# Feed-forward products of a fp32 attention and feed-forward kernel, issued in column pieces of at most 192

## The chip, the cores and the metric

The kernel runs on one core of a Trainium2 chip. The metric is the device time of one execution in microseconds (us); lower is better. Everything is computed in fp32.

## The reference, cut to what matters

An attention block with RMS-normalised queries and keys is followed by a feed-forward block whose inner activation is "SoLU" (h times its softmax) with a layer norm behind it. The change touches only the two large products of the second block, `x @ w_in` and `ln @ w_out`.

```python
# attention: q, k, v of shape (8 batches, 12 heads, 448 positions, 64)
q_n, k_n = rmsnorm(q, g_q), rmsnorm(k, g_k)
attn = softmax(q_n @ k_n.T / sqrt(64))
x = (attn @ v).transpose(0, 2, 1, 3).reshape(3584, 768)

# feed-forward: w_in (768, 1024), w_out (1024, 768)
h = x @ w_in                                    # (3584, 1024)
sm = exp(h - max(h)); sm = sm / (sum(sm) + 1e-9)
solu = h * sm
ln = (solu - mean(solu)) / sqrt(var(solu) + 1e-6) * g_ln
out = ln @ w_out                                # (3584, 768)
```

## The kernel before, in words

The program has a `fast_path` and a `general_path`; a flag computed on the chip decides at the end whether the second is needed as well. With these inputs only the fast path runs, and everything below is about it. Its order of instructions is written out by hand: the body stands under `tc.manual_schedule()`, and small closures (`unit`, `later`, `follow`) place each step of the side engines a fixed number of units behind a step of TensorE.

The work falls into three stages.

1. Attention. Scores (line 771 and 784), exponentials on ScalarE (L761), values (L813, L824) and softmax sums (L843) for 24 groups of four heads. The matmuls here use parts of the array: 64x64 for the scores, 128x64 for the values, 128x32 for the sums. In this stage the weights of the feed-forward part are converted and combined bit by bit. The result x goes out to device memory (`xd`).
2. `x @ w_in`. The 3584 rows are 28 tiles of 128 rows, taken two at a time in NG = 14 groups. Each group's product is a 2x2 block product that is computed with seven block products in place of eight (the Strassen-Winograd scheme): blocks `a11 a12 a21 a22` and their sums `s1` to `s4` against seven weight blocks that were prepared ahead. The row sums are made on GpSimd (`block_sums`, L933 to L937), the results are put together on VectorE (`plus`, L962) and ScalarE (the copy `q1`, L966). Then the softmax and the layer norm of each tile follow on ScalarE, VectorE and GpSimd (`ff_max` to `ff_norm`, L1009 to L1039), and `ff_spread` writes the normalised rows to device memory (`ud`), in an order from which they can be read back transposed.
3. `ln @ w_out`. The same scheme over the same 14 groups. Its stationary operand is read back from `ud` by `load_u` into tiles `uT` of shape `[128, 2, 2, 128, HF]` with HF = 4, so that one contraction chunk of a block is `a[:, :, c]`: 128 columns that lie four fp32 elements apart. The block sums `us` have the same form. In stage 2 the corresponding operand is `a[:, c]` of `xg` or `xsum`: 128 columns one behind the other.

All products of stages 2 and 3 go through one helper, `mul` inside `products`. One call makes one block product. It takes one PSUM bank from a rotation of five (tags `tttoo`, three buffers of `t` and two of `o`) and accumulates over the chunks of the contraction: 3 chunks (HD) in stage 2 with 512 output columns, 4 chunks (HF) in stage 3 with 384 output columns (HO). Per chunk there is one matmul call: the data block (128x128) is stationary, the weights `w[:, i, c]` are moving.

```python
            last = w.shape[2] - 1
            for c in range(last + 1):
                nc.tensor.matmul(
                    o, a[:, c] if kind == "A" else a[:, :, c], w[:, i, c], start=(c == 0), stop=(c == last)
                )
```

In the trace every fp32 matmul call of these stages is a pair of matmul instructions, each with a weight load (LDWEIGHTS) of its own. So stage 2 has 14 groups x 7 products x 3 chunks x 2 = 588 matmul instructions and 588 weight loads, and stage 3 has 14 x 7 x 4 x 2 = 784 of each. Line numbers are those of the kernel before; its matmul call is at L953.

Shortly before the end of stage 3, three small transposes of a 128x1 column (`check_all`, L581, tile `pw`) run on TensorE between two products, for a check of the value range.

Of the kernel before, what the change touches and what calls it, by code (L numbers as in the profile page):

```python
# [366 lines left out]
def fast_path(  # L367
# [24 lines left out]
    nc = tc.nc  # L392
# [546 lines left out]
    def products(g, kind, w, n, c11, c12, c21, c22, done):  # L939


        k = {}

        def mul(a, i):
            a11, a12, a21, a22 = gs[g, kind]
            sm = gs[g, "s" if kind == "A" else "us"]
            a = {"a11": a11, "a12": a12, "s3": a21, "a22": a22, "s1": sm[:, 0], "s2": sm[:, 1], "s4": sm[:, 2]}[a]
            tag = "tttoo"[len(banks) % 5]
            banks.append(tag)
            o = k["o"] = ps_t.tile([P, 512], FP32, tag=tag, name="b", bufs=3 if tag == "t" else 2)[:, 0:n]  # L950
            last = w.shape[2] - 1
            for c in range(last + 1):
                nc.tensor.matmul(  # L953
                    o, a[:, c] if kind == "A" else a[:, :, c], w[:, i, c], start=(c == 0), stop=(c == last)
                )

        def part(name):
            k[name] = second.tile([P, 512], FP32, tag="part", name=name, bufs=4)[:, 0:n]
            return k[name]

        def plus(out, x):
            nc.vector.tensor_tensor(out, k["o"], k[x], OP.add)  # L962

        def p1():
            mul("a11", 0)
            nc.scalar.copy(part("q1"), k["o"])  # L966

        def p6():
            mul("s2", 5)
            plus(part("u2"), "q1")  # L970

        def p2():
            mul("a12", 1)
            plus(c11(), "q1")

        def p7():
            mul("s3", 4)
            plus(part("u3"), "u2")

        def p5():  # L980
            mul("s1", 3)
            plus(c22(), "u3")
            plus(k["u2"], "u2")

        def p4():
            mul("a22", 6)
            plus(c21(), "u3")
            done(1)

        def p3():  # L990
            mul("s4", 2)
            plus(c12(), "u2")
            done(0)

        return [p1, p6, p2, p7, p5, p4, p3]
# [153 lines left out]
    with tc.manual_schedule():  # L1149
# [19 lines left out]
        for m in range(NQ):  # L1169
            a, b = 2 * m, 2 * m + 1  # L1170
# [238 lines left out]
```

## Time and profile before

| | |
|---|---|
| time before, median of 2 runs | 851.29 us (850.75 to 851.82) |
| the profiled execution's own time | 855.39 us |
| its span, first to last instruction | 853.6 us |
| mean granted TensorE clock | 0.998 |
| instructions in the span | 13057 |
| TensorE matmul (PE) | 4432 instructions, busy 830.1 us (97%) |
| TensorE weight loads (PEld) | 4432 instructions, busy 481.6 us (56%) |
| VectorE / ScalarE / GpSimd busy | 616.3 / 375.9 / 323.1 us |
| stage 2, first to last matmul start | 342.34 to 594.37 us |
| stage 3, first to last matmul start | 594.79 to 847.76 us |

How to read it: PE is TensorE's matmuls and PEld its weight loads, which are recorded apart from each other and may overlap. DVE is VectorE, ACT is ScalarE, POOL is GpSimd, SP is SyncE, which issues transfers. The end of a matmul is modelled and two neighbours overlap in the record, so the cost of a matmul in a dense stretch is the distance from its start to the next one's start, not its duration. "L953" is a line of the kernel; a row such as `b<-w_in,xg` says that the instruction writes tile `b` from `w_in` and `xg`.

### The profile page before, as it was taken

How to read it: one execution, taken by the hardware profiler on the slowest of the kernel's cores; microseconds unless marked ns; L12 is line 12 of the kernel's file. 1: busy time of each engine (PE TensorE's matmuls, PEld its weight loads, DVE VectorE, ACT ScalarE, POOL GpSimd, SP SyncE). 2: the span in 40 equal slices, each digit the busy share in tenths (PEclk: the TensorE clock that was granted, in tenths of full speed). 3: DMA queues.
4: the chain of work that ended last, by engine and by line, in shares of the span. 5: the costliest groups of instructions: out<-in, count | busy, mean ns of one | idle time of the engine just before them, and what ended most of it. 6: DMA issues, size and time to landing. Idle time of an engine off the chain costs nothing.

```text
span 853.6 us, 13057 instructions
## 1 busy us (share of the span) xinstructions
PE 830.1 (97%) x4432; PEld 481.6 (56%) x4432; DVE 616.3 (72%) x990; ACT 375.9 (44%) x559; POOL 323.1 (38%) x464
## 2 busy tenths in 40 slices
PE   5999999999999999999999999999999999999997
PEld 2334434333433333444444444445999999999996
DVE  5778988799998889589999999999933333333322
ACT  5677877778787776155445453443200000000000
POOL 1444443546455457222333223554333222233220
PEclk9999999999999999999999999999999999999999
DMA  5677777888767673234443444453564445544331
GB/s 119 138 173 177 171 178 156 181 188 172 175 146 174 135 188 118 73 97 132 109 124 105 128 113 105 135 137 92 153 227 151 151 151 182 179 151 141 119 117 41
DMA packets 268060, 121.63 MB, mean 142 GB/s; under 512 B 190672, under 2 KB 250064, under 8 KB 267984
## 3 DMA queue, kind: packets, MB, share of 16 engines
q1 hardware_dynamic: 253584, 110.65, 50.4%
q10 hardware_dynamic: 14400, 10.06, 4.1%
q8 instruction: 37, 0.61, 0.3%
q14 instruction: 39, 0.32, 0.1%
HBM read 83.96 MB, written 36.70 MB: 141 GB/s over the span
## 4 chain that ended last, share of the span: by engine, by line
PE 67%; DVE 11%; SPq 7%; DMA 7%; ACT 3%; issue 2%; POOL 2%; ACTq 0%; POOLq 0%; DVEq 0%
PE b L953 59%; SPq L610 7%; DVE es L798 3%; PE o L824 3%; PE s L771 2%; DVE qkT L699 2%; DVE part L640 2%; DMA v<-in_v_dram 1%; POOL ss L650 1%; DVE r L869 1%; ACT E L761 1%; DMA qk<-in_k_dram 1%; PE sm L843 1%; DMA raw<-in_moe_w_in_dram 1%; DVE xo L870 1%
## 5 line engine op out<-in xcount | busy, mean ns | idle before, releaser
L953 PE MATMUL b<-w_out,uT 128*128 128x384 f32 x448 | 151.4, 486 | 0.0
L953 PE MATMUL b<-w_in,xg 128*128 128x512 f32 x336 | 151.1, 592 | 0.0
L953 PEld LDWEIGHTS b<-w_out,uT 128*128 128x128 f32 x448 | 138.1, 308 | 6.7 <-issue 0.2
L761 ACT ACTIVATE E<-s 128x896 f32<-128x896 f32 x168 | 138.8, 931 | 4.2 <-PE s L771 3.3
L771 PE MATMUL s<-qkT 64*64 64x448 f32 x1152 | 127.1, 567 | 0.8 <-DVE qkT L754 0.8
L966 ACT COPY q<-b 128x512 f32<-128x512 f32 (+1 forms) x28 | 14.9, 532 | 251.7 <-PE b L953 239.0
L953 PE MATMUL b<-w_out,us 128*128 128x384 f32 x336 | 115.4, 486 | 0.0
L953 PE MATMUL b<-w_in,xsum 128*128 128x512 f32 x252 | 115.0, 592 | 0.0
L824 PE MATMUL o<-E,v 128*64 128x448 f32 x576 | 113.5, 543 | 0.0
L953 PEld LDWEIGHTS b<-w_in,xg 128*128 128x128 f32 x336 | 63.8, 190 | 80.2 <-issue 78.3
L953 PEld LDWEIGHTS b<-w_out,us 128*128 128x128 f32 x336 | 103.5, 308 | 4.8
L689 POOL TENSOR_TENSOR qkn<-qk,ny 128x896 f32<-128x896 f32 x46 | 77.9, 1713 | 31.2 <-DVE ny L680 10.8
L771 PEld LDWEIGHTS s<-qkT 64*64 64x64 f32 x1152 | 45.6, 166 | 67.6 <-ACT E L761 35.7
L953 PEld LDWEIGHTS b<-w_in,xsum 128*128 128x128 f32 x252 | 47.9, 190 | 60.3 <-issue 58.4
L650 POOL COPY ss<-part 32x56 f32<-32x56 f32 x88 | 32.9, 374 | 125.5 <-DVE part L640 122.7
L824 PEld LDWEIGHTS o<-E,v 128*64 128x64 f32 x576 | 39.2, 137 | 72.7 <-issue 61.4
L1033 POOL TENSOR_TENSOR he<-he,mhalf 128x1 f32<-128x1 f32 x28 | 17.6, 630 | 160.1 <-DVE he L1032 159.8
L933 POOL TENSOR_TENSOR us<-uT 128x512 f32<-128x512 f32 x14 | 17.8, 1272 | 149.9 <-DMA uT<-ud 108.9
L962 DVE TENSOR_TENSOR y<-b,u 128x384 f32<-128x384 f32 x42 | 23.4, 557 | 62.0 <-PE b L953 62.0
L798 DVE TENSOR_TENSOR es<-E 128x896 f32<-128x896 f32 x48 | 64.7, 1350 | 0.0
L1039 ACT ACTIVATE u<-u,shift,he 128x1024 f32<-128x1024 f32 x28 | 34.6, 1237 | 63.3 <-POOL shift L1035 63.3
L640 DVE TENSOR_REDUCE part<-sq 128x28 f32<-128x896 f32 x46 | 49.4, 1074 | 13.6 <-ACT sq L632 12.9
(106 smaller groups left out, 1056.5 us busy)
## 6 DMA issues: line engine op xcount, KB each, us to landing
ud<-ub SPq DMA_DIRECT2D x112, 128.0 KB, 2.5
uT<-ud SPq DMA_DIRECT2D x56, 256.0 KB, 4.3
xd<-xo SPq DMA_DIRECT2D x24, 448.0 KB, 3.8
out_dram<-y SPq DMA_DIRECT2D x27, 384.0 KB, 2.6
qk<-in_q_dram SPq DMA_DIRECT2D x184, 56.0 KB, 2.7
qk<-in_k_dram SPq DMA_DIRECT2D x184, 56.0 KB, 2.3
v<-in_v_dram SPq DMA_DIRECT2D x24, 384.0 KB, 5.0
raw<-in_moe_w_in_dram SPq DMA_DIRECT2D x12, 512.0 KB, 4.6
```

The lines of the kernel that those rows point to most:

```text
L610: nc.sync.dma_start(d["qk"][g * 32 : g * 32 + 32, s], src[b, h0 + g // 2].rearrange("(b t) (x d) -> x t b d", t=32, x=2)[g % 2],)
L640: nc.vector.tensor_reduce(norms[m]["part"][:, i], st[n]["sq"], AX, OP.add)
L650: e.tensor_copy(ss[g * 32 : g * 32 + 32], part[o * 32 : o * 32 + 32])
L689: e.tensor_tensor(d["qkn"], d["qk"].rearrange("p s b d -> p (s b) d"), y.rearrange("p b -> p b ()").to_broadcast([P, 2 * NB, 32]), OP.mult,)
L761: nc.scalar.activation(d["E", kc], s[:, :, 0:S], AF.Exp)
L771: nc.tensor.matmul(s[c : c + D, h, 0:S], d["qkT"][hh, 1, keys], d["qkT"][hh, 0, :], start=True, stop=True,)
L798: nc.vector.tensor_tensor(d["es"], d["E", 0], d["E", 1], OP.add)
L824: nc.tensor.matmul(d["o"][h * D : (h + 1) * D, :], quads[n // 2]["v"][:, n % 2 * 2 + h, kc], d["E", kc][:, h], start=False, stop=(kc == NJ ...
L933: nc.gpsimd.tensor_tensor(s1, a21, a22, OP.add)
L953: nc.tensor.matmul(o, a[:, c] if kind == "A" else a[:, :, c], w[:, i, c], start=(c == 0), stop=(c == last))
L962: nc.vector.tensor_tensor(out, k["o"], k[x], OP.add)
L1039: nc.scalar.activation(d["u"], d["u"], AF.Identity, scale=d["e"], bias=d["shift"])
```

## The change

One matmul call over all output columns of a product becomes several over pieces of at most 192 columns: 512 columns are issued as 192, 192 and 128, and 384 columns as 192 and 192. The loop over the pieces is outside and the loop over the contraction chunks inside, so that each piece is accumulated to its end before the next begins. All pieces of a product lie in the same PSUM bank as before, and the buffers, the other engines' instructions and their order are the same.

```diff
@@ -949,10 +949,13 @@
             banks.append(tag)
             o = k["o"] = ps_t.tile([P, 512], FP32, tag=tag, name="b", bufs=3 if tag == "t" else 2)[:, 0:n]
             last = w.shape[2] - 1
-            for c in range(last + 1):
-                nc.tensor.matmul(
-                    o, a[:, c] if kind == "A" else a[:, :, c], w[:, i, c], start=(c == 0), stop=(c == last)
-                )
+            for x in range(0, n, 192):
+                cols = slice(x, min(n, x + 192))
+                for c in range(last + 1):
+                    nc.tensor.matmul(
+                        o[:, cols], a[:, c] if kind == "A" else a[:, :, c], w[:, i, c, cols],
+                        start=(c == 0), stop=(c == last),
+                    )
```

## The prediction

> **What bounds the kernel now.** I read the page's busy times and slices first, then the chain, then the two stages by themselves, then the groups of line 953, and last single instructions in order of time. The busy times and slices:
>
> ```profile
> PE 830.1 (97%) x4432; PEld 481.6 (56%) x4432; DVE 616.3 (72%) x990; ACT 375.9 (44%) x559; POOL 323.1 (38%) x464
> PE   5999999999999999999999999999999999999997
> PEld 2334434333433333444444444445999999999996
> DVE  5778988799998889589999999999933333333322
> ```
>
> TensorE is full from end to end. The second row matters more: weight loads take four tenths of the time in stage 2, and over nine tenths in the last twelve slices, stage 3. The chain, merged, and busy times of the two stages (columns: window, its length, PE, PEld, clock, DMA share, GB/s):
>
> ```profile
> 342.41 497.65 PE b L953 x1348
> ```
> ```profile
> 342.34:594.79 252.45, 252.45 (x588) 111.94 (x589) 1.00 0.42 114
> 594.79:848.25 253.46, 253.29 (x785) 241.29 (x783) 1.00 0.45 147
> ```
>
> From 342 us on the end is set by line 953 alone: 506 us with no gap in which another engine or a transfer could hide anything. Each microsecond that these products gain or lose is one of the kernel. One instruction costs 252.45 / 588 = 429 ns at 512 columns. At 384 columns it is 322.5 ns, start to start in the trace (253.46 less 0.45 for the check at L581, over 784, is the same within 0.3 ns). The groups of the line (out<-in, shape, count | busy, mean ns):
>
> ```profile
> L953 PE MATMUL b<-w_out,uT 128*128 128x384 f32 x448 | 151.4, 486 | 0.0
> L953 PE MATMUL b<-w_in,xg 128*128 128x512 f32 x336 | 151.1, 592 | 0.0
> L953 PEld LDWEIGHTS b<-w_out,uT 128*128 128x128 f32 x448 | 138.1, 308 | 6.7 <-issue 0.2
> L953 PEld LDWEIGHTS b<-w_in,xg 128*128 128x128 f32 x336 | 63.8, 190 | 80.2 <-issue 78.3
> ```
>
> A load of 128 columns is recorded with 190 ns where they lie one behind the other (stage 2) and with 308 ns where they are four elements apart (stage 3). Both now fit under the matmul before: 190 under 429, 308 under 322.5. With 192 columns the second no longer does. How much of a recorded load counts is the question; two places show it. The first matmul of stage 2 begins when TensorE has nothing else, together with its own load (count: min/median/max ns):
>
> ```profile
> L953 PEld LDWEIGHTS b<-w_in,xg x1: 186/186/186, 342.3 to 342.3; 128*128 128x128 f32 x1
> L953 PE MATMUL b<-w_in,xg x1: 697/697/697, 342.3 to 342.3; 128*128 128x512 f32 x1
> ```
>
> It is 697 ns long instead of 592: it waited 105 ns, though its load took 186. The last 80 ns or so of a recorded load lie beside the matmul that uses it. Smaller loads say the same: 132 ns for 64 columns make an L824 matmul 590 instead of 539 ns (51 exposed), 106 ns for 32 columns make an L843 matmul 377 instead of 352 (25 exposed). Stage 3 has one short matmul ahead of a strided load, the check's third transpose (start in us, length; x2 are two instructions; three narrow windows of the timeline):
>
> ```profile
> 840.00 0.38 PE L581 MATMUL pw<-ident,worst 128*1 128x128 f32 x2
> ```
> ```profile
> 840.22 0.93 PE L953 MATMUL b<-w_out,us 128*128 128x384 f32 x2
> ```
> ```profile
> 840.12 0.31 PEld L953 LDWEIGHTS b<-w_out,us 128*128 128x128 f32 x1
> ```
>
> The third transpose, 128 columns, starts at 840.11 (in the trace 840.113; the second at 840.004, so 109 ns each). The strided load starts 2 ns behind it. The product's first matmul starts at 840.223 and is 606 instead of 486 ns long, a wait of 120; the next starts at 840.665. Taking off a regular 322.5, the first really began at 840.343. So a short matmul followed by a strided load held TensorE for 230 ns, where its columns alone need 109: 308 less 80, plus 2.
>
> **What the Trainium skill says.** "TensorE: Matmul & The Clock Gate", section "Back-to-back issue gap": spacing is columns over the clock plus 2.5 ns, for one pass. Here two cycles go to each column and the constant fits: 429, 322.5 and 109 ns at 512, 384 and 128 columns lie on 2.3 ns + 0.833 ns per column. The same page, "LDWEIGHTS": a load takes its columns over 1.2, which is 107 ns for 128. The exposed 105 agrees; the recorded 190 doesn't, and of a stride the page says nothing, where this trace shows 118 ns more. The same page, "Step-by-step": the next weights load while this matmul runs. The trace agrees, and shows the limit: in dense stretches each load starts 2 ns after the start of the matmul before its own, never one matmul earlier. "Perfetto Trace Analysis", section "Identifying the Most-Contended Engine", warns that matmul busy time says little and weight-load busy time more: 95% in stage 3 is that warning.
>
> **The change part by part.** The number of columns streamed is the same; the number of instructions isn't. Successive instructions have different weight blocks (the chunk loop is inside), so every piece needs its load again. Stage 2 goes from 588 matmuls with loads to 1764, stage 3 from 784 to 1568.
>
> *Price of a piece.* It is the larger of the streaming time and the load's hold. Streaming: 192 columns, 2.3 + 160 = 162.3 ns; 128 columns, 109 ns. Hold of an adjacent load: 105 to 110 + 2 = 107 to 112 ns. Hold of a strided load: 230 ns as seen once; the load after that one began 17 ns before the real start of its predecessor and was recorded with 330 instead of 308 ns, which by the same reckoning gives 330 - 17 - 80 = 233. I take 232.
>
> *Stage 2.* 192, 192, 128 columns: 162.3 + 162.3 + 109 = 433.6 ns against 429, so 4.6 x 588 = 2.7 us. If the hold of 112 decides the last piece, 1.8 us more; I leave that in the range.
>
> *Stage 3.* 2 x 232 = 464 ns against 322.5, so 141.5 x 784 = 110.9 us. All of it is on the path: nothing else ends there.
>
> *The rest.* The readers of a product (L962, L966) wait for its last matmul as before; they come late by what the product lasts longer and have idle time to take it: DVE is busy 94 of 253 us in stage 3, and 231 of 255 in stage 2, which grows by only 1%. The PSUM rotation of five banks comes free no later relative to TensorE. The 3920 extra TensorE instructions have to be fetched; the instruction queues now take 0.4% of the DMA time, and half as much again would not show. These go at nothing; if an engine did come late, one group's products in stage 2 last 18 us and its VectorE work 16.5, so what could come late is bounded by a few microseconds at the stage's end.
>
> *Sum.* 2.7 + 110.9 = 113.6 us. On the profiled execution's own 855.39 us (span 853.6 and 1.8 around it) that gives 969.0. The median of the runs shown is 4.1 lower, and from it 964.9. Forecast: **965 us**, slower by 13%.
>
> Own range of this case: the lowest hold is the strided load without the fixed part that the 1-column load at L581 shows (84 ns): 308 - 84 = 224, so 125.5 x 784 + 2.7 = 101 and 952 us. The highest is 330 - 80 + 2 = 252 in every piece, (504 - 322.5) x 784 = 142 us, with 4.5 us for stage 2: 147, and 998 us. A few microseconds on the low side for run to run make it 945 to 1000.
>
> **The rivals.**
>
> *The whole recorded load counts.* If in a dense row of short matmuls the overlap of 80 ns is lost, a piece costs 310 ns in stage 3 and 192 in stage 2: (620 - 322.5) x 784 = 233 and (576 - 429) x 588 = 86, together 1171 us. For it: recorded loads of 308 fill the present 322.5 so closely. Against it: 840.22 shows 230, and 342.34 shows 105.
>
> *The load hides after all (the other side: not slower).* If the 118 ns that the stride adds are delay and not occupancy, consecutive strided loads could follow each other within 160 ns, and stage 3 would stay bound by its columns: 324.6 against 322.5, 1.6 us, with stage 2 together 4 us, 856 us. It decides from a hold of 162 ns downwards, in stage 3. For it: a second adjacent load at the start of the program ends 106 ns after the first, so fixed parts do overlap. Against it: the wait of 120 at 840.22, which already had 110 ns of load behind it.
>
> *The clock falls.* TensorE streams only 162 of each 232 ns in stage 3; if the clock then halved, a piece would take 320 ns: (640 - 322.5) x 784 = 249 us, 1103 us. For it: the first 16 us show matmuls at half pace (746 ns for 448 columns, later 376). Against it: those follow idle time, and here TensorE never rests longer than 70 ns.
>
> That the pieces don't reach TensorE, or share their loads, is excluded by the order of the changed kernel's instructions (192, 192, 128 columns, each over all chunks) and by the loop order.
>
> **How the numbers follow.** The forecast's case 0.83; whole load 0.07; hidden load 0.04; clock 0.03; something between (holds of 255 to 300) 0.03. The likeliest case gives 965. Its own range and a little above it, 945 to 1005, leaves less than 2 in 10 outside. Slower by over 2% in all but the hidden case: 0.95; within 2%: 0.04; faster by over 2%: 0.01, since nothing is taken away. 2% is about what a measurement of this kernel can tell from no change.
>
> **What would show it.** In the changed profile stage 3 should have 1568 matmuls of 192 columns some 232 ns apart and last about 364 us, with PEld near full; stage 2 1764 matmuls, about 255 us; attention unchanged, up to 342 us. A stage 3 of 255 us would show that the stride is delay, one of 485 that the whole load counts, and a stage 2 near 340 the same for adjacent loads; a clock below 1 in stage 3 would be the third rival.

## The result, and the profile after

The changed kernel takes 974.49 us (972.13 to 976.85, 2 runs) against 851.29 us: a ratio of 1.141 with a 95% interval of 1.136 to 1.147. It is slower by 14%; 965 us had been forecast. The profiled execution took 972.13 us with a span of 970.2, against 855.39 and 853.6 before.

The page's busy times and slices of the kernel after, the same rows as those shown of before:

```profile
PE 944.9 (97%) x6392; PEld 752.0 (78%) x6392; DVE 616.5 (64%) x990; ACT 376.4 (39%) x559; POOL 322.8 (33%) x464
PE   6899999999999999999999999999999999999997
PEld 2334444433333399999999999999999999999997
DVE  5778888899889958999999989622222222222212
```

TensorE has 1960 matmuls and as many weight loads more, and its busy share is 97% as before. Only the second row shows that its time is spent otherwise: weight loads now fill both stages of the products, not just the last. VectorE's work is the same to 0.2 us, spread over a longer span.

The chain, merged, and then busy times by stage (window, its length, PE, PEld, DVE, ACT, POOL, clock, DMA share, GB/s), from the first start of each stage:

```profile
341.54 611.67 PE b L955 x3284
953.54 11.27 PE b L955 x48
```
```profile
341.47:598.33 256.86, 256.86 (x1768) 256.86 (x1765) 227.82 (x352) 108.69 (x169) 91.58 (x125) 1.00 0.42 113
598.33:964.80 366.47, 366.47 (x1573) 366.09 (x1571) 98.70 (x187) 11.18 (x20) 66.53 (x56) 1.00 0.31 102
```

Stage 2 starts at 341.47 us, within 1 us of before. From its first matmul start to that of stage 3 it lasts 256.86 us against 252.45, and stage 3 lasts 366.06 against 252.97 from first to last matmul start. That is 4.4 + 113.1 = 117.5 us, less 0.9 us in which attention was shorter: the whole difference of the spans, 116.6 us. From 341.5 us on the chain has only the matmul line and, between the two entries shown, the three transposes of the check. The clock is 1.00.

The groups of the line after (count | busy, mean ns of one):

```profile
L955 PE MATMUL b<-w_out,uT 128*128 128x192 f32 x896 | 216.0, 397 | 0.0
L955 PEld LDWEIGHTS b<-w_out,uT 128*128 128x128 f32 x896 | 213.1, 329 | 0.0
L955 PE MATMUL b<-w_in,xg 128*128 128x192 f32 x672 | 118.6, 326 | 0.0
L955 PEld LDWEIGHTS b<-w_in,xg 128*128 128x128 f32 x1008 | 150.1, 191 | 0.4 <-issue 0.4
```

Where adjacent columns are loaded, in stage 2, a matmul of 192 columns is recorded with 326 ns; in stage 3 it has 397, so 71 ns of it are waiting. Busy time over count gives about the cost of one: 216.0 / 896 = 241 ns, a little too much, since each unbroken run of such matmuls ends with a full recorded length. The trace's start times give 233.4 ns on average over 1566 distances (the one across the check is left out), and 99% of them are 233 or 234.

### The profile page after: what moved, and what is told of

Read it like the earlier page. It is cut to its first block, busy times and chain, and to the rows that moved or that the text cites. A ratio compares the mean times of both kernels' runs of the same rounds, so it can differ in the third digit from the quotient of the medians.

```text
span 970.2 us, 16991 instructions
## 1 busy us (share of the span) xinstructions
PE 944.9 (97%) x6392; PEld 752.0 (78%) x6392; DVE 616.5 (64%) x990; ACT 376.4 (39%) x559; POOL 322.8 (33%) x464
## 4 chain that ended last, share of the span: by engine, by line
PE 76%; SPq 8%; DMA 5%; DVE 4%; ACT 3%; issue 2%; POOL 1%; ACTq 0%; POOLq 0%; DVEq 0%
PE b L955 64%; SPq L610 7%; PE o L824 4%; PE s L771 4%; PE sm L843 2%; DMA qk<-in_k_dram 1%; DVE es L798 1%; ACT sq L632 1%; DMA raw<-in_moe_w_out_dram 1%; ACT E L761 1%; DVE part L640 1%; DMA qk<-in_q_dram 1%; DVE qkT L699 1%; PE s L784 1%; PE o L813 1%
## 5 line engine op out<-in xcount | busy, mean ns | idle before, releaser
L955 PE MATMUL b<-w_out,uT 128*128 128x192 f32 x896 | 216.0, 397 | 0.0
L955 PEld LDWEIGHTS b<-w_out,uT 128*128 128x128 f32 x896 | 213.1, 329 | 0.0
L955 PE MATMUL b<-w_out,us 128*128 128x192 f32 x672 | 163.7, 397 | 0.0
L955 PEld LDWEIGHTS b<-w_out,us 128*128 128x128 f32 x672 | 160.8, 329 | 0.0
L955 PE MATMUL b<-w_in,xg 128*128 128x192 f32 (+1 forms) x1008 | 153.7, 309 | 0.0
L955 PEld LDWEIGHTS b<-w_in,xg 128*128 128x128 f32 x1008 | 150.1, 191 | 0.4 <-issue 0.4
L771 PE MATMUL s<-qkT 64*64 64x448 f32 x1152 | 124.4, 558 | 0.8 <-DVE qkT L754 0.8
L955 PE MATMUL b<-w_in,xsum 128*128 128x192 f32 (+1 forms) x756 | 116.9, 309 | 0.0
L955 PEld LDWEIGHTS b<-w_in,xsum 128*128 128x128 f32 x756 | 113.4, 191 | 0.0
L965 DVE TENSOR_TENSOR u<-b,q 128x512 f32<-128x512 f32 (+1 forms) x28 | 17.5, 626 | 85.6 <-PE b L955 82.0
```

What stands on the lines that cost most here:

```text
L771: nc.tensor.matmul(s[c : c + D, h, 0:S], d["qkT"][hh, 1, keys], d["qkT"][hh, 0, :], start=True, stop=True,)
L955: nc.tensor.matmul(o[:, cols], a[:, c] if kind == "A" else a[:, :, c], w[:, i, c, cols], start=(c == 0), stop=(c == last),)
```

## The experiments

The theory to be tested: a matmul in a dense row costs the larger of two things, the time to stream its columns (2.3 ns + 0.833 ns per column) and the hold of its weight load (112 ns adjacent, 233 ns four apart). Two rivals: A, a fixed cost of every added matmul; B, narrow pieces stream badly whatever the load. Windows below are those of stages 2 and 3 or of stage 3 alone, columns as above; each is taken from the stage's first matmul start and includes its tail.

**One part of the change alone: stage 2.**

```diff
-            for x in range(0, n, 192):
-                cols = slice(x, min(n, x + 192))
+            step = 192 if kind == "A" else n
+            for x in range(0, n, step):
+                cols = slice(x, min(n, x + step))
```

> Pieces of 192, 192, 128 in the first product alone (stage 2); the second product (stage 3) whole as before. Theory (a matmul costs the larger of its streaming time and its weight load's hold, 112 ns for adjacent columns and 233 ns for columns four apart): stage 2 grows from 252.0 to about 256.7 us, the time to about 856 us. Rival A (every added matmul costs a fixed 59 ns, which is the whole loss of 116.6 us over 1960 added matmuls): 1176 x 59 ns = 70 us more, about 921 us.

Measured: 863.03 us (860.11 to 864.3, 5 runs) beside 856.22 us of the kernel before on the same chip; the ratio is 1.008 (1.007 to 1.010).

```profile
342.46:599.33 256.87, 256.87 (x1768) 256.86 (x1765) 227.79 (x352) 108.59 (x169) 91.61 (x125) 1.00 0.42 113
599.33:852.90 253.57, 253.57 (x789) 241.85 (x787) 98.12 (x187) 11.28 (x20) 66.56 (x56) 1.00 0.45 146
```

Stage 2 alone has the changed kernel's 256.9 us, stage 3 is untouched. Rival A's 921 us is far off. The forecast of the absolute time, 856 us, was low by 7, of which 5 are the level of that series: there the kernel before took 856 too.

**The other part alone: stage 3.**

```diff
-            for x in range(0, n, 192):
-                cols = slice(x, min(n, x + 192))
+            step = n if kind == "A" else 192
+            for x in range(0, n, step):
+                cols = slice(x, min(n, x + step))
```

> Pieces of 192, 192 in the second product alone (stage 3); the first whole. Theory: stage 3 goes from 253.0 to about 366 us (1568 x 233 ns), the time to about 965 to 970 us, nearly all of the change's loss. Rival A (59 ns for every added matmul): 784 x 59 ns = 47 us more, about 898 us.

Measured: 970.61 us (964.54 to 970.97, 4 runs), ratio 1.131 (1.128 to 1.135).

```profile
596.59:962.93 366.34, 366.34 (x1572) 365.96 (x1570) 98.63 (x187) 11.37 (x20) 66.60 (x56) 1.00 0.31 102
```

The loss sits in stage 3. The two parts add up: they take 6.8 us and 114.4 us over 856.22 in this series, together 121.2 beside 123.2 for the whole change. In their profiles the stages grew by 4.4 and 113.0 us.

**The suspected cost taken away: the stride.** Counts, pieces and waits stay; only the addresses of the stationary columns change.

```diff
+            flat = a.rearrange("p t c -> p (t c)") if kind == "U" else None
-                        o[:, cols], a[:, c] if kind == "A" else a[:, :, c], w[:, i, c, cols],
+                        o[:, cols], a[:, c] if kind == "A" else flat[:, c * P : (c + 1) * P], w[:, i, c, cols],
```

> The changed kernel, but stage 3 takes as its stationary block 128 columns that lie one behind the other in the same tile, in place of 128 columns four elements apart. It multiplies other elements than the reference does; counts, shapes, buffers, waits and the pieces are those of the changed kernel. Theory: recorded loads fall from 329 to about 190 ns, the hold to 112 ns, a piece is bound by its 192 columns again (163 ns), stage 3 lasts about 256 us, the time is about 858 us. Rival A (fixed cost of an added matmul) and rival B (narrow pieces stream badly whatever the load): no change, about 974 us.

Measured: 864.28 us (859.56 to 869.16, 4 runs), ratio to the kernel before 1.011 (1.008 to 1.014).

```profile
596.06:851.40 255.34, 255.30 (x1573) 254.87 (x1571) 98.14 (x188) 11.31 (x20) 66.51 (x56) 1.00 0.45 146
```
```profile
L956 PEld LDWEIGHTS b<-w_out,uT 128*128 128x128 f32 x896 | 146.7, 190 | 0.0
L956 PE MATMUL b<-w_out,uT 128*128 128x192 f32 x896 | 152.5, 326 | 0.0
```

This settles that the stride is the cause. With the same 1568 matmuls and loads, stage 3 is back at 255 us: loads 190 instead of 329 ns, matmuls 326 instead of 397, 162.5 ns from start to start. Rivals A and B both had 974. PEld still reads as busy nearly the whole time (254.87 of 255.34): its busy share alone doesn't say that loads are what the engine waits for.

**The stride's price by size.** Three apart, in pieces of 192 (`flat[:, c : c + 3 * P - 2 : 3]`):

> The changed kernel, but stage 3 takes 128 columns three elements apart (other elements than the reference's; all else the same). Theory with the stride's price read from the score loads of before (64 columns three apart 161 ns against about 130 adjacent, so 62 ns more for 128): recorded load about 252 ns in a sparse stretch, hold about 177 ns, stage 3 about 278 us, time about 880 us. If the price grew evenly with the stride (118 ns / 3 per step): hold about 194, stage 3 about 304 us, about 906 us. Rivals A and B: about 974 us.

Measured: 879.31 us; one execution.

```profile
595.72:872.07 276.35, 276.29 (x1573) 275.92 (x1571) 98.31 (x188) 11.29 (x20) 66.66 (x56) 1.00 0.41 135
```

The price read from a smaller load of another stage was right: 175.9 ns from start to start for 177 expected, and 276 us of stage 3 for 278. That the whole time agrees within a microsecond is partly luck, since attention alone moves a single time by more. The even price per step, 906 us, is out.

Pieces of 96 make the hold visible where it is below 162 ns. First with the stride of four as it is:

```diff
-            for x in range(0, n, 192):
-                cols = slice(x, min(n, x + 192))
+            step = n if kind == "A" else 96
+            for x in range(0, n, step):
+                cols = slice(x, min(n, x + step))
```

> First product whole; second product in pieces of 96 columns (four to a product, 3136 matmuls in stage 3), loads of columns four apart as in the changed kernel. Theory (the hold of 233 ns goes with each load, however few columns follow it): stage 3 = 3136 x 233 ns = 731 us, time about 1330 us. Rival A in its remaining form (each added matmul costs what one cost in the second product, 113 us over 784 = 144 ns): 2352 x 144 = 339 us more, about 1195 us. Rival B (each column of a narrow piece costs 233 / 192 = 1.21 ns): no more than with 192, about 968 us.

Measured: 1338.26 us; one execution.

```profile
345.77:598.23 252.46, 252.46 (x592) 111.94 (x589) 227.59 (x352) 108.68 (x169) 91.70 (x125) 1.00 0.43 114
598.23:1330.48 732.25, 732.25 (x3140) 731.94 (x3138) 98.63 (x187) 11.37 (x20) 66.51 (x56) 0.50 0.16 51
```

3136 loads at 233.3 ns, the same as with twice the columns behind each: the cost goes with the load. Rivals A (1195) and B (968) miss by over 100 us. The clock column was not expected: half speed for nearly the whole of stage 3.

Then two apart (`flat[:, c // 2 * 2 * P + c % 2 : c // 2 * 2 * P + c % 2 + 2 * P - 1 : 2]`) and adjacent (`flat[:, c * P : (c + 1) * P]`):

> As the kernel with pieces of 96 in the second product, but with stationary columns two elements apart (other elements than the reference's). The pieces are short enough for the hold to show. If the read of a load goes with the bytes it spans (0.44 ns per element of stride, from 1.31 ns per column at three and 1.75 at four, but never below 0.83 ns): recorded load about 200 ns, hold about 120 ns, stage 3 = 3136 x 120 = 376 us, time about 975 us. If the price of the stride grows evenly (39 ns per step): hold about 150 ns, stage 3 about 470 us, time about 1070 us.

> As the kernel with pieces of 96 in the second product, but with adjacent stationary columns (other elements than the reference's). Theory: streaming 96 columns takes 82 ns, the hold of an adjacent load 112 ns decides, stage 3 = 3136 x 112 = 351 us, time about 950 us. If adjacent loads hid below 112 ns: 3136 x 82 = 258 us, about 856 us.

Measured: 972.86 us and 952.89 us; one execution each. Stage 3 of the two, in this order:

```profile
595.81:965.60 369.79, 369.79 (x3140) 369.56 (x3138) 98.65 (x187) 11.35 (x20) 66.58 (x56) 1.00 0.31 101
```
```profile
594.78:945.50 350.72, 350.63 (x3140) 350.40 (x3138) 98.71 (x188) 11.33 (x20) 66.47 (x56) 1.00 0.33 107
```

From start to start that is 117.8 and 111.6 ns. All four holds of a 128-column fp32 load, as start-to-start times of the trace where the load decides:

| columns apart (fp32 elements) | 1 | 2 | 3 | 4 |
|---|---|---|---|---|
| hold, ns | 111.6 | 117.8 | 175.9 | 233.3 |
| recorded length of the load, ns | 192 | 196 | 263 | 329 |

A step of two costs 6 ns and each further one 57 to 58. From two to four apart the hold goes with the elements spanned: 0.45 ns for each of the 256, 384 or 512, and about 3 ns beside. Adjacent columns lie above that line, as if there were a floor of about 0.85 ns per column. This is a fit to four numbers, all of fp32 blocks; what in the read makes it so is not shown.

**Where the larger of the two changes over.** Pieces of 256 and 128, then of 320 and 64 (`step = n if kind == "A" else 256`, and `320`):

> First product whole; second product in pieces of 256 and 128 columns. Theory (a piece costs the larger of its streaming time, 215.6 and 109 ns, and the hold of 233 ns): 233 + 233, the same as 192 and 192: stage 3 = 366 us, time about 968 us. If streaming and load added up in part, so that a longer piece costs more: each ns on the 256-column piece is 0.8 us.

> First product whole; second product in pieces of 320 and 64 columns, so that the first piece is above the hold and the second far below. Theory: 269 + 233 = 502 ns per pair, stage 3 = 784 x 502 = 394 us, time about 996 us. Rival (only the number of loads counts): 366 us, about 968 us. Streaming is busy for 324 of 502 ns (65%), so the clock should stay at 1.0.

Measured: 969.14 us and 1000.48 us; one execution each.

```profile
595.75:962.00 366.25, 366.24 (x1572) 365.96 (x1570) 98.62 (x187) 11.39 (x20) 66.57 (x56) 1.00 0.31 102
```
```profile
599.36:993.25 393.89, 393.89 (x1572) 393.70 (x1570) 98.60 (x187) 11.38 (x20) 66.52 (x56) 1.00 0.29 95
```

256 and 128 columns cost what 192 and 192 do, since neither reaches the hold. At 320 the first piece streams for 269 ns and the second still pays 233. Stage 3 is 394 us as worked out. A piece costs the larger of the two; the cost is neither their sum nor a count of loads.

**Do pieces with the same stationary block share a load?** The loops exchanged:

```diff
-            for x in range(0, n, 192):
-                cols = slice(x, min(n, x + 192))
-                for c in range(last + 1):
+            for c in range(last + 1):
+                for x in range(0, n, 192):
+                    cols = slice(x, min(n, x + 192))
...
-                        start=(c == 0), stop=(c == last),
+                        start=(c == 0 and x == 0), stop=(c == last and x + 192 >= n),
```

> The changed kernel with its two loops exchanged: for each chunk of the contraction all pieces in a row, so that successive matmul calls have the same stationary block. Theory (every matmul instruction brings its own weight load, and the two passes of a call have loads of their own): 1568 loads in stage 3 as before, 366 us, time about 974 us. Rival (a load of the block that is already there is left out or costs nothing): stage 3 about 256 to 310 us, time 860 to 915 us.

Measured: 976.67 us; one execution.

```profile
603.06:969.52 366.46, 366.46 (x1573) 366.09 (x1571) 98.70 (x187) 11.18 (x20) 66.59 (x56) 1.00 0.31 102
```

They don't. There are 1568 loads as before, each with a hold of 233.4 ns. The order of the loops is no remedy. This speaks of fp32 calls as they are issued here, each a pair of matmul instructions with loads of their own.

**Is the stride worth anything in the kernel before?** Whole products with adjacent columns (the `flat` of above, `step = n`):

> The kernel before (products whole) with adjacent stationary columns in the second product (other elements than the reference's). Theory: 322.5 ns of streaming hide either load, so stage 3 stays at 253.0 us and the time at about 854 us: the stride costs nothing until the pieces are cut. If the strided load already took part in the present 322.5 ns, stage 3 falls below 253 us.

Measured: 850.82 us; one execution.

```profile
590.39:843.73 253.34, 253.34 (x788) 148.94 (x786) 98.04 (x187) 11.48 (x20) 66.36 (x56) 1.00 0.45 147
```

Stage 3 is 252.85 us from first to last start instead of 252.97: nothing, though the loads' busy time in it fell from 241 to 149 us. A loaded PEld row was no cost as long as each load fitted under the matmul ahead of it: the 95% that the prediction read as a warning became 59%, and the stage took the same time. No variant here has shorter product stages than the kernel before, beyond 0.2 us.

## Why the prediction was right

*What sets the end.* Line 953 alone from 342 us on: that held. Attention moved by 0.9 us, and the readers on the other engines never set the end; the chain after is TensorE's from there on.

*How much of a load counts.* The step that everything hung on was to take 80 ns off the recorded 308, from a single strided load at 840 us and the one behind it, and not to charge the whole load (1171 us). It gave 232 ns; 1568 loads showed 233.4. The overlap of 80 ns is the same in the dense row of the changed kernel. There, counted in ns from the recorded start of one matmul, the next load starts at 55 and lasts 329, so it ends at 384; the matmul that uses it is recorded from 233 on and waits 71, so it really begins at 304, 80 before the load's end.

By recorded lengths the prediction's reading was incomplete: 190 ns do not fit under the 162.3 of a 192-column piece either, and stage 2 stayed cheap because only 112 of them count. The rival that the stride is only delay had 856 us and fell with the measured time; that the addresses are the cause is shown by the pair of kernels that differ in them alone (974 and 864 us).

*Sizes.* Stage 3 was worked out as 110.9 us and measured 113.1, of which 1568 x 1.4 ns = 2.2 is the hold. Stage 2 was worked out as 2.7 and measured 4.4: the last piece was priced at its streaming time of 109 ns, and it took 111 to 112. There the load decides after all, by 2 to 3 ns, as the prediction left to its range (2.7 + 1.8 = 4.5). On the profiled execution's own time the sum gave 969.0 and 972.13 was measured.

*The term that was off most* is not one of the change: from the profiled execution to the median, 4.1 us were taken off because the kernel before had shown that; the changed kernel's median lies 2.4 us above its profiled run. That is 6.5 of the 9.5 us of the miss. Across the profiled runs, stage 2 begins anywhere from 337.9 to 346.9 us in attention code that is the same, while stages 2 and 3 repeat within 0.2 us; so single times carry several microseconds that belong to attention. What makes attention vary is not known.

*The clock.* The outcome was right (1.00 with 192 columns), but the reason given, that TensorE never rests longer than 70 ns, is not one that the runs bear out. With 96 columns and a hold of 233 ns the rest is some 150 ns, and the clock halved 4 us into the stage. With pieces of 320 and 64 the rest behind a piece of 64 is longer, 178 ns, eight times in a row, and the clock stayed. What fits all these runs is the share of streaming at full speed: 162 of 233 ns (70%), 82 of 118 (70%) and 324 of 502 (65%) kept the clock; 82 of 233 (35%), seen in one execution, lost it. Where between 35 and 65% it turns was not tried.

## What to carry to other kernels

Before cutting matmuls into smaller ones, compare the streaming time of a piece with the hold of its weight load, for each operand layout by itself: the same cut of 384 columns into 192 and 192 cost 0.8% of stage 3 with adjacent stationary columns (254.97 against 252.97 us) and 45% with columns four apart. The hold is the recorded load less what overlaps its own matmul, and can be read off any matmul that waits for its load. Where short moving pieces can't be avoided, lay the stationary columns side by side or at most two elements apart (tried here with fp32 blocks of 128 columns); where a piece streams longer than the hold, that rearrangement is worth nothing.

## What the runs showed of the hardware that the prediction did not have

- The step from two to three elements apart: 111.6, 117.8, 175.9 and 233.3 ns for one to four. A stride of two is nearly free.
- TensorE's granted clock fell to 0.50 for 707 us when its columns needed 35% of the time at full speed, in a row of instructions with no gap in the record. It cost nothing that the runs show: the hold was 233.3 ns there and 233.4 in the changed kernel at full clock. By estimate, 96 columns at half speed take some 160 ns (746 ns for 448 columns in the first 16 us), which still lies under the hold.
- A load that decides is recorded longer than one that doesn't, 329 ns instead of 308, and in the changed kernel it starts some 16 ns before the matmul ahead of it really begins. Its hold is 233: its recorded duration is not its cost.
